# The 32x32 corner of a cross network's tail: from a padded weight tile to two small tiles read straight from the tail weights

## The chip, the cores and the metric

The kernel runs on one core of one Trainium2 chip. The metric is the device time of one execution in microseconds (us). The chip's engines are called PE (TensorE, matrix multiply; PEld is its loading of weights), DVE (VectorE), ACT (ScalarE), POOL (GpSimd) and SP (SyncE, which issues most of the DMAs).

## What is computed

```python
B, F, D, L = 4096, 26, 16, 6
Din = min(F * D, 1024)            # 416
...
def reference(x0, ws, bs):        # x0 [4096, 416], ws [6, 416, 416], bs [6, 416], all bf16
    x = x0
    for l in range(ws.shape[0]):
        x = x0 * (x @ ws[l] + bs[l]) + x
    return x
```

Since the bias enters every layer, the kernel keeps the state divided by x0 in its head: each layer's sum x @ W + b + (all earlier sums) + 1 stays in the accumulators (PSUM), and x is that sum times x0.

## The kernel before, in words

The state is held transposed, features on partitions. The 416 features are three chunks of 128 and a tail of 32 (DF = 384, DR = 32). The 4096 rows are taken in NS = 4 blocks of 1024 rows, and each block in two halves of 512 (h = 0, 1). For each block s and layer l the loop at the end of the kernel emits, in this order: the main matmuls of half 0 (`main`, 128x32 tiles: 128 rows of features, and the 32 output features of one quarter of a chunk in each of the four column strips), the tail block (`tail_rows`), the evictions of half 0 by VectorE (`leave`, L417), the tail outputs (`tail_outs`, from 384 main features to the 32 tail features), the tail's own eviction (`leave_tail`: ScalarE L427, a product on GpSimd L440, then swaps by ScalarE L404 and GpSimd L406), then the main matmuls and evictions of half 1. The last layer of the last block is done by rows of x and has no such tail block, so there are 23 of them.

The tail features are 32, a quarter of the partitions, so the tail of 1024 rows is folded: four groups q of G = 256 rows stand one above the other, group q on partitions 32q to 32q + 31 (`quad(q)`). Each tail tile has a second plane, in which neighbouring groups (q and q ^ 1) are swapped. With both planes a row group sees the two halves of 512 rows: even q takes both planes as one stretch of 512 columns, odd q takes them one after the other as two matmuls of 256.

`tail_rows` has two parts, each one step of the plan with one semaphore at its end. `first` holds row tiles (32x128: 32 tail features in, 128 features out) into the accumulators of chunks 0 and 1. `second` has the row tiles of chunk 2 on even groups and the corner, tail to tail, on odd groups. The corner multiplies by the 32x32 piece `wt_sb[..., DF:D]` of the tail weights; its outputs have to land on the partitions of the group whose rows they are. Before the change a padded copy does this: `wc_sb` holds, for each layer and each of two parts, a 32x128 tile that is zero but for the 32 columns of the wanted group, so that the corner too is a 32x128 matmul. The memset at L249 clears `wc_sb` and `corner` (L251) copies the pieces in on GpSimd: layer 0 ahead of the loop (L529), layer 1 after layer 0's tail (L561), layers 2 to 5 after layer 1's (L563). The accumulators of the tail are banks 6 and 7 (`T_BANK`): the partitions 0 to 63 of bank 6 and 64 to 127 of bank 7 are used.

The order of work is written by hand; the class `Plan` only derives the semaphores from the named reads and writes. All matmuls of the layers go through `mm` (L261, recorded as L262). `tail_in` transposes the next block's tail features into the upper columns of bank 6 in layer 2.

Of the kernel before, what the change touches and what calls it, by code (L numbers as in the profile page):

```python
# [118 lines left out]
def bass_standalone__dcn_v2_cross__recsys_kernel(  # L119
# [6 lines left out]
    B, D = x0.shape  # L126
    L = ws.shape[0]
    NC = 3
    DF = 128 * NC
# [5 lines left out]
    G = SB // 4  # L135
    JS = SB // 128
    NJ = B // 128
    T_BANK = (6, 7)
# [3 lines left out]
    with ExitStack() as es:  # L142

        def sb(name, shape, dt=BF16):
            return es.enter_context(nc.sbuf_tensor(name, shape, dt))

        w_sb = sb("w_sb", [128, L, NC, D])
        wt_sb = sb("wt_sb", [128, L, D])
        wc_sb = sb("wc_sb", [128, L, 2, 128])
        xin_sb = sb("xin_sb", [128, 4, D])  # L150
        xtl_sb = sb("xtl_sb", [128, NJ, DR])
        xr_sb = sb("xr_sb", [128, JS, D])
# [19 lines left out]
        ps = es.enter_context(nc.psum_tensor("ps", [128, 8, 512], FP32))  # L172
# [5 lines left out]
        P = Plan()  # L178

        def quad(q):  # L180
            return slice(32 * q, 32 * q + 32)
# [44 lines left out]
        for s in range(1, NS):  # L226
# [7 lines left out]
            writes=[("dummy",)],  # L234
# [3 lines left out]
                out=ident[:, :], in_=ones_sb[:, 0:128], pattern=[[-1, 128]],  # L238
# [6 lines left out]
                out=u_sb[:, :], in_=ones_sb[0:L + 1, 0:L], pattern=[[1, L]],  # L245
                compare_op=ALU.is_ge, fill=0.0, base=1, channel_multiplier=-1,
            ), reads=[("ones",)], writes=[("u",)],
        )
        P.add("gpsimd", lambda e: e.memset(wc_sb[:, :, :, :], 0.0), writes=[("wc", "wt%d" % i) for i in range(3)])  # L249

        def corner(a, b, name):  # L251
            for g in range(4):
                p = quad(g | 1)
                P.add(
                    "gpsimd", lambda e, p=p, g=g: e.tensor_copy(  # L255
                        out=wc_sb[p, a:b, g % 2, quad(g)], in_=wt_sb[p, a:b, DF:D]
                    ), reads=[("wt", name), ("wc", name)], writes=[("wc", name, g)], shifts=True,
                )


        def mm(pe, dst, lhsT, rhs, start, pos=None):  # L261
            return pe.matmul(  # L262
# [14 lines left out]
        def wkey(l):  # L277
            return "wt%d" % min(l, 2)
# [29 lines left out]
        def tail_rows(s, l, start):  # L308
            src, key = src_tail(s, l)
            keys = [("wt", wkey(l)), key, key + ("swapped",)]  # L310

            def rows(pe, q, h, m, begin):
                for part in range(2):
                    if q % 2 == 0:
                        if part:
                            break
                        dst, rhs = ps[:, bank(h, m), :], src[quad(q), :, :]
                    else:
                        dst, rhs = ps[:, bank(h, m), part * G:(part + 1) * G], src[quad(q), 1 - part, :]
                    ins = mm(  # L320
                        pe, dst, wt_sb[quad(q), l, m * 128:(m + 1) * 128], rhs, begin and part == 0, (32 * q, 0)
                    )
                return ins

            def first(pe):
                for q in range(4):
                    h, m = divmod(q, 2)
                    ins = rows(pe, q, h, m, l == 0 and h == 1)
                return ins

            def second(pe):
                for q in range(4):
                    h = q // 2
                    if q % 2 == 0:
                        ins = rows(pe, q, h, 2, l == 0 and h == 1)
                    else:
                        for part in range(2):
                            ins = mm(
                                pe, ps[:, T_BANK[h], 0:G], wc_sb[quad(q), l, part, :], src[quad(q), 1 - part, :],
                                start and part == 0, (32 * q, 0),  # L340
                            )
                return ins

            P.add("tensor", first, reads=keys, adds=[("ps", bank(h, m)) for h in HALVES for m in range(2)])
            P.add(
                "tensor", second, reads=keys + [("wc", wkey(l), g) for g in range(4)],
                adds=[("ps", bank(h, 2)) for h in HALVES] + [("ps", T_BANK[h]) for h in HALVES],
            )

# [17 lines left out]
        def tail_in(s):  # L367
            def fn(pe):
                for o in range(2 if s == 0 else 1):
                    for r in range(2):  # L370
                        for g in range(4):
                            j = 2 * (g ^ o) + r
                            src = xin_sb[:, j, DF:D] if s == 0 and j < 4 else xtl_sb[:, s * JS + j, :]
                            b, c = (7, o * G) if s == 0 else (T_BANK[0], G)
                            ins = mm(
                                pe, ps[quad(g), b, c + r * 128:c + (r + 1) * 128], src, ident[:, :],
                                s == 0 and o == 0 and r == 0, (0, 32 * g),
                            )
                return ins

            b = 7 if s == 0 else T_BANK[0]
            P.add(
                "tensor", fn, reads=[("ident",), ("xtl", 0 if s == 0 else 1)] + ([("xin", 0), ("xin", 1)] if s == 0 else []),
                adds=[("ps", b)],
            )
            if s == 0:
                P.add(
                    "scalar", lambda e: e.activation(  # L388
                        out=x0t_sb[:, s, :, :], in_=ps[:, 7, :].rearrange("p (o c) -> p o c", o=2), func=ACTF.Copy
                    ), reads=[("ps", 7)], writes=[("x0t", s), ("x0t", s, "swapped")],  # L390
                )
# [90 lines left out]
        for i in range(2):  # L482
            for c in CH:
                b = HEAD_BANKS[i][c]
# [10 lines left out]
                dst, src = x0T_sb[:, c, i * 256:(i + 1) * 256], psT[:, b, 0:256]  # L495
# [30 lines left out]
            )  # L526


        corner(0, 1, "wt0")  # L529
        for s in range(NS):  # L530
            for l in range(L):
                ending = s == NS - 1 and l == L - 2
                if s == NS - 1 and l == L - 1:
                    break
                if s == 0 and l == 0:
                    for k in CH:
                        for m in CH:
                            main(s, l, 0, m, k)
                        if k == 0:
                            bias_sums()  # L540
                        if k == 1:
                            tail_in(0)
                    tail_rows(s, l, True)
                    for c in CH:
                        leave(s, l, 0, c)
                    tail_outs(s, l, False)
                else:
                    for m in CH:
                        for k in CH:
                            main(s, l, 0, m, k)  # L550
                    tail_rows(s, l, l == 0)
                    for c in CH:
                        leave(s, l, 0, c)
                    tail_outs(s, l, False)
                if l == 2 and s < NS - 1:
                    tail_in(s + 1)
                leave_tail(s, l, not ending)
                if l == 2 and s < NS - 1:
                    keep_tail_in(s + 1)
                if s == 0 and l == 0:  # L560
                    corner(1, 2, "wt1")  # L561
                if s == 0 and l == 1:
                    corner(2, L, "wt2")  # L563
                if l == 1 and s > 0:
                    store_block(s - 1)
                if s < NS - 1 and l in (3, 4):
                    g = 2 * (l - 3)
                    swap(x0t_sb[:, s + 1], ("x0t", s + 1), tuple("scalar" if q // 2 == l - 3 else None for q in range(4)))
                if ending:
                    P.add(  # L570
                        "gpsimd", lambda e: e.tensor_tensor(
                            out=bt_sb[:, :], in0=cb_sb[:, NC, L - 1:L], in1=cb_sb[:, NC, L - 2:L - 1], op=ALU.subtract
                        ), reads=[("cb",)], writes=[("bt",)],
                    )
                    P.add(
                        "gpsimd", lambda e, t=t32_sb[:, l % 2, :]: e.tensor_scalar_add(st_sb[:, :], t, bt_sb[:, :]),
                        reads=[("t32", l % 2), ("bt",)], writes=[("st",)],
                    )
                    for c in CH:
                        keep_sum(0, c, "scalar")  # L580
                for m in CH:
                    for k in CH:
                        main(s, l, 1, m, k)
                    leave(s, l, 1, m)
                if ending:
                    for c in CH:
                        keep_sum(1, c, ("scalar", "scalar", "vector")[c])
            if s < NS - 1:
                transpose_block(s)
# [131 lines left out]
```

## Time and profile before

| | |
|---|---|
| runs, median (lowest to highest) | 129.16 us (128.88 to 129.17) |
| the profiled execution | 129.15 us, of which the span is 127.9 us |
| granted clock of TensorE | 1.00 |
| PE | busy 124.4 us, 2426 matmuls |
| DVE | busy 98.2 us |
| ACT | busy 50.1 us |
| POOL | busy 39.6 us |
| corner matmuls (wc_sb) | 92, 268 ns each |
| copies into wc_sb, memset | 12 of 0.2 to 0.3 us, 1.37 us |

The profile lists, for one execution, groups of instructions (line, engine, operation, output and inputs, shape of the tile as rows*columns, count), the waits between engines, the chain of work that ended last, and a timeline in which neighbouring instructions of one kind are merged into a line: its start, its length, and how many there are. The length of a matmul's record is not the time it occupies the engine: the records of a stream overlap, and their ends are modelled. What a matmul costs is read from the distance between the starts.

### The profile page before, as it was taken

To read this page: it belongs to the slowest core of one execution; us is meant where nothing else is said; L and a number is where in the kernel's file an instruction comes from. 1 tells how busy PE (TensorE), PEld (TensorE's weight loads), DVE (VectorE), ACT (ScalarE), POOL (GpSimd) and SP (SyncE) were. 2 spreads that over 40 slices of the span, in tenths; PEclk is the share of its full clock that TensorE was granted. 3 is DMA by queue.
4 is the path that set the end of the run, shared out by engine and by line. 5 is a ranking of instruction groups with operands and counts; after the bars stand their busy time and mean duration, and the time that the engine had idled before them with its cause. 6 is when DMAs were issued, how large, how long until landed. Compare 5 with 4: busy or idle time off the path is not lost.

```text
span 127.9 us, 5334 instructions
## 1 busy us (share of the span) xinstructions
PE 124.4 (97%) x2426; PEld 64.7 (51%) x2426; DVE 98.2 (77%) x150; ACT 50.1 (39%) x112; POOL 39.6 (31%) x88
## 2 busy tenths in 40 slices
PE   7999999999999999999999999999999999999991
PEld 5545445545545545545545545545555555455660
DVE  0329779679779779788788797797797797797973
ACT  1534226356405224354513243373422252253820
POOL 7025364034014053043122152241221351340550
PEclk9999999999999999999999999999999999999999
DMA  3987999997739307000019208000009606100016
GB/s 106 205 201 175 161 262 273 172 204 149 253 67 143 65 19 258 5 0 5 0 33 192 52 0 265 7 5 0 5 0 129 142 5 233 38 0 5 0 38 233
DMA packets 34054, 13.12 MB, mean 103 GB/s; under 512 B 25322, under 2 KB 34032, under 8 KB 34032
## 3 DMA queue, kind: packets, MB, share of 16 engines
q1 hardware_dynamic: 33328, 12.25, 45.8%
q10 hardware_dynamic: 704, 0.54, 1.3%
q8 instruction: 19, 0.31, 1.0%
q14 instruction: 3, 0.02, 0.0%
HBM read 4.07 MB, written 3.41 MB: 58 GB/s over the span
## 4 chain that ended last, share of the span: by engine, by line
PE 97%; ACT 0%; DVE 0%; issue 0%
PE ps L262 93%; PE ps L270 2%; PE ps L488 1%; ACT x0t_sb L388 0%; DVE o_sb L652 0%
## 5 line engine op out<-in xcount | busy, mean ns | idle before, releaser
L417 DVE SCALAR_TENSOR_TENSOR xT_sb<-ps,cb_sb,x0T_sb 128x512 bf16<-128x512 f32 x120 | 80.8, 743 | 19.5 <-PE ps L262 19.5
L262 PE MATMUL ps<-xT_sb,w_sb 128*32 128x512 bf16 (+1 forms) x1596 | 84.6, 364 | 0.0
L262 PEld LDWEIGHTS ps<-xT_sb,w_sb 128*32 128x32 bf16 x1596 | 40.8, 97 | 37.2 <-issue 4.0
L427 ACT ACTIVATE t_sb<-ps,cb_sb 64x256 f32<-64x256 f32 x46 | 21.6, 470 | 51.3 <-PE ps L262 51.0
L440 POOL TENSOR_TENSOR xt_sb<-t_sb,x0t_sb 128x256 bf16<-128x256 f32 x20 | 13.4, 672 | 64.1 <-ACT t_sb L427 64.1
L404 ACT ACTIVATE xt_sb<-xt_sb 32x256 bf16<-32x256 bf16 x38 | 15.7, 414 | 15.3 <-POOL xt_sb L440 15.1
L262 PE MATMUL ps<-x0T_sb,w_sb 128*32 128x512 bf16 (+1 forms) x336 | 18.9, 368 | 0.0
L406 POOL COPY xt_sb<-xt_sb 32x256 bf16<-32x256 bf16 x38 | 14.9, 392 | 2.4
L417 DVE SCALAR_TENSOR_TENSOR xo_sb<-ps,cb_sb,x0T_sb 128x512 bf16<-128x512 f32 x18 | 12.1, 743 | 2.5 <-PE ps L262 2.5
L262 PEld LDWEIGHTS ps<-x0T_sb,w_sb 128*32 128x32 bf16 x336 | 8.4, 97 | 7.6 <-issue 0.6
L262 PE MATMUL ps<-xt_sb,wt_sb 32*128 32x512 bf16 (+1 forms) x152 | 11.8, 326 | 0.0
L262 PE MATMUL ps<-xt_sb,wc_sb 32*128 32x256 bf16 x76 | 7.4, 268 | 0.0
L262 PEld LDWEIGHTS ps<-xt_sb,wt_sb 32*128 32x128 bf16 x152 | 2.5, 91 | 8.4 <-DVE xT_sb L417 6.4
L440 POOL TENSOR_TENSOR xot_sb<-t_sb,x0t_sb 128x256 bf16<-128x256 f32 x3 | 2.0, 672 | 9.9 <-ACT t_sb L427 9.9
L262 PE MATMUL ps<-w_sb,xT_sb 128*32 128x416 bf16 (+1 forms) x60 | 5.1, 339 | 0.0
L404 ACT ACTIVATE x0t_sb<-x0t_sb 32x256 bf16<-32x256 bf16 x12 | 4.9, 410 | 0.1
L652 DVE TENSOR_TENSOR o_sb<-ps,xr_sb 128x416 bf16<-128x416 f32 x6 | 3.4, 588 | 1.3 <-PE ps L262 1.0
L255 POOL COPY wc_sb<-wt_sb 32x32 bf16<-32x32 bf16 (+1 forms) x12 | 2.8, 233 | 4.7 <-DMA wt_sb<-in_ws_dram 4.1
L270 PE MATMUL ps<-const-bfloat16-1.0 128*128 128x256 bf16 x14 | 3.1, 418 | 0.8 <-PEq L706 0.8
L262 PEld LDWEIGHTS ps<-xt_sb,wc_sb 32*128 32x128 bf16 x76 | 3.7, 93 | 0.2
L503 DVE COPY x0T_sb<-ps 128x256 bf16<-128x256 bf16 x4 | 1.1, 292 | 3.4 <-PE ps L488 3.2
L449 ACT ACTIVATE sS_sb<-ps,cb_sb 128x512 bf16<-128x512 f32 x5 | 3.0, 692 | 0.0
(41 smaller groups left out, 33.6 us busy)
## 6 DMA issues: line engine op xcount, KB each, us to landing
out_dram<-o_sb SPq DMA_DIRECT2D x3, 832.0 KB, 4.4
w_sb<-in_ws_dram SPq DMA_DIRECT2D x5, 312.0 KB, 4.3
xr_sb<-in_x_dram SPq DMA_DIRECT2D x1, 832.0 KB, 5.3
wt_sb<-in_ws_dram SPq DMA_DIRECT2D x4, 104.0 KB, 2.9
out_dram<-o_sb SPq DMA_DIRECT2D x2, 208.0 KB, 2.2
w_sb<-in_ws_dram SPq DMA_DIRECT2D x3, 104.0 KB, 3.4
xin_sb<-in_x_dram ACTq DMA_DIRECT2D x1, 208.0 KB, 3.2
xin_sb<-in_x_dram SPq DMA_DIRECT2D x1, 208.0 KB, 2.9
```

The source lines that it names most:

```text
L255: "gpsimd", lambda e, p=p, g=g: e.tensor_copy(out=wc_sb[p, a:b, g % 2, quad(g)], in_=wt_sb[p, a:b, DF:D]), reads=[("wt", name), ("wc", nam ...
L262: return pe.matmul(dst, lhsT=lhsT, rhs=rhs, start=start, stop=True, skip_group_check=True, tile_position=pos,)
L270: ins = pe.matmul(ps[:, 7, 0:256], lhsT=const[:, 0:128], rhs=const, start=True, stop=True)
L404: fn = lambda e, d=dst, s=src: e.activation(out=d, in_=s, func=ACTF.Copy)
L406: fn = lambda e, d=dst, s=src: e.tensor_copy(out=d, in_=s)
L417: "vector", lambda e: e.scalar_tensor_tensor(out=dst, in0=ps[:, bank(h, c), :], scalar=cb_sb[:, c, l:l + 1], in1=x0T_sb[:, c, o:o + H], op ...
L427: "scalar", lambda e, p=p, h=h: e.activation(out=dst[p, :], in_=ps[p, T_BANK[h], 0:G], func=ACTF.Identity, bias=cb_sb[p, NC, l:l + 1]), re ...
L440: "gpsimd", lambda e: e.tensor_tensor(out=dst, in0=t, in1=x0t_sb[:, s, 0, :], op=ALU.mult),
L449: fn = lambda e: e.activation(out=o, in_=i, func=ACTF.Identity, bias=b)
L488: ins = pe.transpose(out=psT[:, b, j * 128:(j + 1) * 128], in_=xin_sb[:, 2 * i + j, c * 128:(c + 1) * 128], identity=ident[:, :],)
L503: "vector", lambda e, d=dst, s=src: e.tensor_copy(out=d, in_=s),
L652: "vector", lambda e: e.tensor_tensor(out=o_sb[:, jj, :], in0=ps[:, b, 0:D], in1=xr_sb[:, j, :], op=ALU.mult), reads=[("ps", b), ("xr",)], ...
```

## The change

The padded tile, its memset and its copies go. The corner is four 32x32 matmuls per tail block, whose weights are read straight from the tail weights: the tile position (32q, 32g) takes row group q as input and puts the result into the column strip of group g. In `second` the order of the groups becomes 0, 2, 1, 3, so that both row tiles of the even groups come before the four corner matmuls. As a corner matmul now writes only the 32 partitions of its group, and no longer zeros to the other 96, `tail_in` sets its start flag for the groups 2 and 3 of bank 6 itself.

```diff
-        wc_sb = sb("wc_sb", [128, L, 2, 128])
...
-        P.add("gpsimd", lambda e: e.memset(wc_sb[:, :, :, :], 0.0), writes=[("wc", "wt%d" % i) for i in range(3)])
-
-        def corner(a, b, name):
-            for g in range(4):
-                p = quad(g | 1)
-                P.add(
-                    "gpsimd", lambda e, p=p, g=g: e.tensor_copy(
-                        out=wc_sb[p, a:b, g % 2, quad(g)], in_=wt_sb[p, a:b, DF:D]
-                    ), reads=[("wt", name), ("wc", name)], writes=[("wc", name, g)], shifts=True,
-                )
...
             def second(pe):
-                for q in range(4):
+                for q in (0, 2, 1, 3):
                     h = q // 2
                     if q % 2 == 0:
                         ins = rows(pe, q, h, 2, l == 0 and h == 1)
                     else:
-                        for part in range(2):
+                        for o in range(2):
+                            g = q ^ o
                             ins = mm(
-                                pe, ps[:, T_BANK[h], 0:G], wc_sb[quad(q), l, part, :], src[quad(q), 1 - part, :],
-                                start and part == 0, (32 * q, 0),
+                                pe, ps[quad(g), T_BANK[h], 0:G], wt_sb[quad(q), l, DF:D], src[quad(q), o, :],
+                                start, (32 * q, 32 * g),
                             )
                 return ins
...
             P.add(
-                "tensor", second, reads=keys + [("wc", wkey(l), g) for g in range(4)],
+                "tensor", second, reads=keys,
...
-                                s == 0 and o == 0 and r == 0, (0, 32 * g),
+                                o == 0 and r == 0 and (s == 0 or g >= 2), (0, 32 * g),
...
-        corner(0, 1, "wt0")
...
-                if s == 0 and l == 0:
-                    corner(1, 2, "wt1")
-                if s == 0 and l == 1:
-                    corner(2, L, "wt2")
```

## The prediction

> **What bounds the kernel now.** I read the page's engine row first, then the chain that ended last, then the timeline of TensorE, and last the waits. Page, engine row and chain:
>
> ```profile
> PE 124.4 (97%) x2426; PEld 64.7 (51%) x2426; DVE 98.2 (77%) x150; ACT 50.1 (39%) x112; POOL 39.6 (31%) x88
> ...
> PE 97%; ACT 0%; DVE 0%; issue 0%
> PE ps L262 93%; PE ps L270 2%; PE ps L488 1%; ACT x0t_sb L388 0%; DVE o_sb L652 0%
> ```
>
> TensorE is busy for 97% of the span, and the chain is TensorE for 97%; its order in time shows one unbroken piece of line 262 from 8.27 us to 125.27 us. Granted clock is 1.00 there (view by stretches). So after 8.27 us whatever TensorE takes longer or shorter goes into the end one for one, unless another engine becomes late. VectorE, next in line, works six evictions of 743 ns per layer (4.46 us) in a layer period of 4.88 us (start of one tail block to the next, 57.43 to 62.31 us below).
>
> The question is the tail block, of which there are 23 (four blocks of 1024 rows by six layers, less the last layer, which is done by rows). Timeline of TensorE from 57 to 67.5 us, start and length in us:
>
> ```profile
> 57.98 4.40 PE L262 MATMUL ps<-xT_sb,w_sb 128*32 128x256 bf16 x84
> 62.31 0.60 PE L262 MATMUL ps<-xt_sb,wt_sb 32*128 32x512 bf16 x7
> 62.54 0.27 PE L262 MATMUL ps<-xt_sb,wc_sb 32*128 32x256 bf16 x1
> 62.54 0.37 PE L262 MATMUL ps<-xt_sb,wt_sb 32*128 32x512 bf16 x1
> 62.55 0.38 PE L262 MATMUL ps<-xt_sb,wc_sb 32*128 32x256 bf16 x3
> 62.86 2.45 PE L262 MATMUL ps<-xT_sb,w_sb 128*32 128x256 bf16 x48
> ```
>
> The reader is to see that the block lasts 0.55 us (62.31 to 62.86) and that the four wc matmuls cost no time of their own: they start at 62.54 and 62.55 with the row tiles of the even groups and run in the row groups that those leave free. The single records of this block, in ns from the first (62310): row tiles 0, 3, 10, 13, then the second halves of the odd groups at 123 and 133; the second part's row tiles of 512 columns at 226 and 236, wc at 232 and 242, and wc again at 341 and 351; the first main matmul at 549.
>
> **What a column costs.** Quartets of main matmuls without a change of shape start 215.7 ns apart at 512 columns and 109 ns at 256. The slope is 106.7/256 = 0.417 ns a column: 107 ns for 256 columns, 213 ns for 512, and some 2 ns besides.
>
> **What a change of tile shape costs.** The records start late wherever the next matmul has another tile shape than the one before. TensorE around the bias sums (128x32 tiles, then 7x32, then 128x32) and near the end (32x128, then 128x128):
>
> ```profile
> 5.87 0.38 PE L262 MATMUL ps<-x0T_sb,w_sb 128*32 128x512 bf16 x4
> 6.19 0.26 PE L262 MATMUL ps<-u_sb,bsa_sb 7*32 7x6 bf16 x16
> 6.37 0.40 PE L262 MATMUL ps<-x0T_sb,w_sb 128*32 128x512 bf16 x4
> ```
>
> ```profile
> 122.18 0.18 PE L262 MATMUL ps<-ident,st_sb 32*128 32x32 bf16 x4
> 122.30 0.53 PE L262 MATMUL ps<-w_sb,xT_sb 128*128 128x416 bf16 x2
> ```
>
> From the last record before, plus its columns, to the first after: 128x32 to 32x128, 61998 + 213 to 62310, 99 ns (98 or 99 in all 22 tail blocks that wait for nothing else); 32x128 to 128x32, 62661 + 107 to 62859, 91 ns (90 or 91 in all 23); 128x32 to 7x32, 5880 + 213 to 6189, 96 ns; 7x32 to 128x32, 6287 to 6377, some 88 ns (this one has a load to wait for too); 32x128 to 128x128, 122197 + 13 to 122302, 92 ns. Besides, the first round after a change is 10 to 12 ns longer: 120 instead of 109 ns (62859 to 62979), 226 instead of 216 ns (6377 to 6603). A tile of 7 rows by 32 columns in one strip of rows is the nearest that this trace has to a 32x32 tile.
>
> **The change part by part.** *The corner matmuls.* Four per block before and after, 256 columns each, four weight loads before and after. Their tile was 32x128, like the row tiles beside them; now it is 32x32. They come after both even row tiles, so the block gets one more change of shape, 32x128 to 32x32, and leaves from 32x32 instead of from 32x128. No change from 32x128 to 32x32 is in this trace. Bounds: at the one end it costs nothing and the corners run beside the 512-column row tiles, as wc does; at the other it costs what the dearest change costs, 99 ns, with nothing beside it. I take 92 ns, in the middle of the five kinds seen (88 to 99 ns), since every change of shape that the trace shows unmasked has it, whether the rows alone change (bias sums, 122.30 us) or rows and columns. That only the number of columns changes here is the weak point.
>
> Block after, in ns from its first record: even row tiles at 226 and 236 as before; their columns end at 236 + 213 = 449; the change, 92, gives 541; the four corners start 3 to 4 ns apart, the last at 551 (the four bias matmuls start at 6189, 6192, 6196, 6199); 107 for its columns and 11 for the first round after a change, 669; the change to the main tiles, 91, gives 760. Before it was 549: 211 ns longer. That the four corners share one stretch of 107 ns, though each has its own moving data, I take from the tail outputs of the 48 matmuls at 62.86 us: quartets with four different sources at 109 ns each. The price by the lowest and highest of the rows: gap in 90, no longer first round and a gap out of 65 (the 88 less the 23 to 25 ns that the small bias matmuls may themselves take) gives 236 + 213 + 90 + 10 + 107 + 65 = 721, 172 ns longer; gap in 99, corners spread over 14 ns and a first round of 12 gives 236 + 213 + 99 + 14 + 107 + 12 + 91 = 772, 223 ns longer. Over 23 blocks: 211 ns is 4.85 us, with 3.96 and 5.13 us as ends.
>
> *The Trainium skill* speaks on this from both sides, and the sum above needs neither. Its page "TensorEngine Tiling (Array Packing)", section "Key Properties", says that a change of tiling mode, and not only of the tile, drains TensorE; the gaps above agree for the changes they show, the page gives no price, and by it the corners would come out as in my sum, near 133.8 us. Its page "TensorE: Matmul & The Clock Gate", section "Part 3: Packing small matmuls — row/col tiling", says that weight loads overlap running matmuls when their row groups differ; read by itself that would let the corners of groups 1 and 3 run beside the row tiles of groups 0 and 2, and the sum would be near 128.8 us.
>
> *The copies that go.* GpSimd loses a memset (1.37 us) and twelve copies (2.8 us). Nearly all of it lies in GpSimd's idle time, between the swaps and the next product, which waits for ScalarE. Two of TensorE's waits name it:
>
> ```profile
> PEld ps L262 <- POOL wc_sb L255: 0.7, 2, 0.4
> ```
>
> That figure is idle time of the weight loads, partly behind matmuls. In the records, the block at 18.03 us has its second part 371 ns after its first instead of 226: it waits for the four copies of layers 2 to 5 (17.00 to 18.34 us). From the main quartet before to the first main matmul after, it lasts 1022 instead of 871 ns; the block at 13.15 us 877 instead of 871; the block at 8.27 us waits for ScalarE, not for the copies. Gain 0.151 + 0.006 = 0.157 us. Nothing takes the place of this wait: the first part of each block waits for the same tail weights already, and they had landed when the copies began (17.00 us at the latest, block at 18.03). Without the copies' wait the second part is bound by its row groups.
>
> *No cost and no gain:* the start flags in tail_in (same matmuls), the freed buffer, the new order of the second part. Its semaphore goes up some 0.2 us later within the block, but VectorE first works the two banks of the first part (1.49 us from 62.77 us), so the third bank is ready in time. The tail outputs, and behind them ScalarE's and GpSimd's tail chain, shift with TensorE; the swaps before the block at 62.31 us end at 61.85 us, and the period gets longer, not shorter. No DMA is moved.
>
> **Sum.** The profiled execution took 129.15 us (span 127.9 and 1.25 around it), the median of the runs is 129.16. 129.15 + 4.85 - 0.16 = 133.84; I say 133.8 us.
>
> **Rivals.** *The corners hide (not slower).* Place: the change from 32x128 to 32x32 in the second part. If it has no gap, the corners run in row groups 1 and 3 beside the 512-column tiles, and the block ends with those: 236 + 213 + 91 = 540 instead of 549. That gives 23 x 9 = 0.21 us and 0.16 from the copies, 128.8 us. For it: the row groups are free, wc does so today, and the trace has no unmasked change of columns alone. Against: five kinds of change, five gaps. It decides when a block grows by less than 7 ns (0.157 us / 23); from there on the kernel is slower.
>
> *The corners follow without a gap.* They wait for the row tiles, but the change is free: 107 ns a block, 2.46 us, 131.4 us. Against: no gap below 65 ns at any change in the records.
>
> *The two corners of one row group go one after the other.* Another 107 ns a block, 2.46 us: 136.3 us. Against: the tail outputs' quartets at 109 ns.
>
> *The change does nothing*, since wc is hidden now and only the 0.16 us are to be had: this is the first rival less its 9 ns, 129.0 us, and counted with it.
>
> **How the numbers follow.** Gaps as in my sum 0.78 (own range 133.0 to 134.2); follow without a gap 0.07; hidden 0.12; one after the other 0.03. The range goes from 131.4 to 134.5 us: it takes in the first two and leaves out the last two, 0.15, and a little of my own case. A measurement can tell about 0.3% (0.39 us) from no change; 128.8 lies just on this edge, so of the 0.12 I give 0.04 to faster and 0.08 to the same; slower 0.88.
>
> **What would show it.** Right: in each block the corner matmuls, as 32*32 tiles, start some 300 ns after the even row tiles (62.54 us today for both), and the next main matmul some 0.21 us after the four; block length 0.76 instead of 0.55 us; layer period 5.09 instead of 4.88 us; clock at 1.00; no block at 18 us with a longer stretch than its neighbours. Wrong: corners that start within 20 ns of the even row tiles (hidden), at 215 ns after them (no gap), or in two steps 107 ns apart (one after the other). VectorE's idle time should grow by some 0.2 us a layer; if TensorE instead waits for VectorE or ScalarE, the one-for-one step was wrong.

## The result, and the profile after

The changed kernel takes 134.06 us (median of 6 runs, 133.5 to 134.13) against 129.25 us (6 runs, 128.88 to 129.65): a ratio of 1.0347, 95% interval 1.0321 to 1.0373. The forecast was 133.8 us, the range 131.4 to 134.5. The profiled execution took 134.10 us, its span 132.8 us (before 129.15 and 127.9), the clock 1.00 in both.

Page of the changed kernel: engine row, chain and VectorE's evictions (busy, mean ns, idle before and its releaser); below it the evictions of the kernel before. The lines that were L262 and L417 are now L250 and L406.

```profile
PE 128.3 (97%) x2426; PEld 61.8 (47%) x2426; DVE 98.1 (74%) x150; ACT 50.0 (38%) x112; POOL 35.5 (27%) x75
...
PE 92%; DMA 3%; SPq 1%; ACT 0%; DVE 0%; issue 0%
...
L406 DVE SCALAR_TENSOR_TENSOR xT_sb<-ps,cb_sb,x0T_sb 128x512 bf16<-128x512 f32 x120 | 80.9, 743 | 24.1 <-PE ps L250 24.1
```

```profile
L417 DVE SCALAR_TENSOR_TENSOR xT_sb<-ps,cb_sb,x0T_sb 128x512 bf16<-128x512 f32 x120 | 80.8, 743 | 19.5 <-PE ps L262 19.5
```

The same 2426 matmuls, and TensorE as full as before at 97%: a busy share says nothing of a stall between matmuls, since the records overlap. VectorE does the same work and waits longer for TensorE (24.1 us; 19.5 before), so TensorE is still what everybody waits for. The chain now begins with a load of the head (DMA 3%), which is another matter, below.

The tail block, timeline of TensorE (start, length):

```profile
64.64 0.83 PE L250 MATMUL ps<-xt_sb,wt_sb 32*128 32x512 bf16 x12
65.40 2.45 PE L250 MATMUL ps<-xT_sb,w_sb 128*32 128x256 bf16 x48
```

It lasts 0.76 us, 0.55 before. All twelve matmuls are merged into one line, and the line bears the name of the first form only. A window that begins behind the ends of the row tiles' records shows the corners by themselves, here for TensorE and then for its weight loads; the third view is of the weight loads before:

```profile
65.18 0.29 PE L250 MATMUL ps<-xt_sb,wt_sb 32*32 32x256 bf16 x4
65.40 0.29 PE L250 MATMUL ps<-xT_sb,w_sb 128*32 128x256 bf16 x4
```

```profile
65.18 0.10 PEld L250 LDWEIGHTS ps<-xt_sb,wt_sb 32*32 32x32 bf16 x4 [0.42 <-issue]
65.40 0.12 PEld L250 LDWEIGHTS ps<-xT_sb,w_sb 128*32 128x32 bf16 x8
```

```profile
62.30 0.12 PEld L262 LDWEIGHTS ps<-xt_sb,wt_sb 32*128 32x128 bf16 x8 [0.42 <-DVE xT_sb L417]
62.43 0.21 PEld L262 LDWEIGHTS ps<-xt_sb,wc_sb 32*128 32x128 bf16 x4
62.85 0.23 PEld L262 LDWEIGHTS ps<-xT_sb,w_sb 128*32 128x32 bf16 x12 [0.21 <-issue]
```

The four corners start at 65.18, 0.3 us behind the even row tiles (64.87), and the main matmuls 0.22 us behind them. Their loads too come only at 65.18, after 0.42 us in which no weights were loaded and nothing that the profile names was waited for ("issue"). Before, the corners' loads (wc_sb) began at 62.43, while row tiles ran. Single records, ns from the block's first:

```
                        rows, 1st part    odd, 2nd half   even rows, 2nd part   corner               main
before (62.31 us)       0 3 10 13         123 133         226 236               232 242 341 351      549
after  (64.64 us)       0 3 10 13         122 132         226 236               540 544 547 550      759
```

Over the 23 blocks the time from a block's first record to the first main matmul sums to 12.786 us before and 17.450 after, 4.664 us more. All else behind the first block is the same: the 22 stretches between blocks 95.57 and 95.58 us, and from the last block's end to the start of the last matmul 8.41 us in both. The first block starts at 8.27 and 8.45 us. So the 4.9 us in the span are 4.66 from the blocks and 0.18 from the head, with rounding.

### The profile page after: what moved, and what is told of

Its sections match the earlier page's. It is cut to its first block, busy times and chain, and to the rows that moved or that the text cites. A ratio compares the mean times of both kernels' runs of the same rounds, so it can differ in the third digit from the quotient of the medians.

```text
span 132.8 us, 5313 instructions
## 1 busy us (share of the span) xinstructions
PE 128.3 (97%) x2426; PEld 61.8 (47%) x2426; DVE 98.1 (74%) x150; ACT 50.0 (38%) x112; POOL 35.5 (27%) x75
## 4 chain that ended last, share of the span: by engine, by line
PE 92%; DMA 3%; SPq 1%; ACT 0%; DVE 0%; issue 0%
PE ps L250 92%; DMA xtl_sb<-in_x_dram 3%; SPq L187 1%; ACT x0t_sb L377 0%; DVE o_sb L636 0%
## 5 line engine op out<-in xcount | busy, mean ns | idle before, releaser
L406 DVE SCALAR_TENSOR_TENSOR xT_sb<-ps,cb_sb,x0T_sb 128x512 bf16<-128x512 f32 x120 | 80.9, 743 | 24.1 <-PE ps L250 24.1
L250 PE MATMUL ps<-xT_sb,w_sb 128*32 128x512 bf16 (+1 forms) x1596 | 84.6, 364 | 0.0
L250 PEld LDWEIGHTS ps<-xT_sb,w_sb 128*32 128x32 bf16 x1596 | 40.8, 97 | 35.5
L250 PE MATMUL ps<-x0T_sb,w_sb 128*32 128x512 bf16 (+1 forms) x336 | 18.6, 365 | 0.2 <-DVE x0T_sb L492 0.2
L250 PE MATMUL ps<-xt_sb,wt_sb 32*128 32x512 bf16 (+2 forms) x228 | 15.7, 310 | 0.0
L406 DVE SCALAR_TENSOR_TENSOR xo_sb<-ps,cb_sb,x0T_sb 128x512 bf16<-128x512 f32 x18 | 12.1, 744 | 3.1 <-PE ps L250 3.1
L250 PEld LDWEIGHTS ps<-x0T_sb,w_sb 128*32 128x32 bf16 x336 | 8.4, 97 | 7.3 <-DVE x0T_sb L492 0.4
L250 PEld LDWEIGHTS ps<-xt_sb,wt_sb 32*128 32x128 bf16 (+1 forms) x228 | 4.2, 90 | 16.1 <-issue 16.1
L250 PE MATMUL ps<-w_sb,xT_sb 128*32 128x416 bf16 (+1 forms) x60 | 5.1, 339 | 0.0
L250 PE MATMUL ps<-x0t_sb,wt_sb 32*128 32x512 bf16 (+2 forms) x48 | 3.3, 310 | 0.1
L250 PEld LDWEIGHTS ps<-w_sb,xT_sb 128*32 128x32 bf16 (+1 forms) x60 | 2.2, 97 | 1.4 <-issue 0.2
L647 POOL TENSOR_TENSOR o_sb<-f_sb,xr_sb 128x416 bf16<-128x416 f32 x2 | 1.9, 974 | 2.9 <-ACT f_sb L643 2.9
```

The source lines that it names most:

```text
L250: return pe.matmul(dst, lhsT=lhsT, rhs=rhs, start=start, stop=True, skip_group_check=True, tile_position=pos,)
L406: "vector", lambda e: e.scalar_tensor_tensor(out=dst, in0=ps[:, bank(h, c), :], scalar=cb_sb[:, c, l:l + 1], in1=x0T_sb[:, c, o:o + H], op ...
L647: "gpsimd", lambda e: e.tensor_tensor(out=o_sb[:, jj, :], in0=t, in1=xr_sb[:, j, :], op=ALU.mult),
```

## The experiments

The two theories throughout: a change of tile shape stalls TensorE for some 92 ns, adds 11 ns to its first round, and nothing runs across it; or it is the small corner tiles themselves, their order or their columns that cost.

**Alternating: three changes more.** The changed kernel with

```diff
-                for q in (0, 2, 1, 3):
+                for q in range(4):
```

> The changed kernel with the groups of the second part in the order 0, 1, 2, 3, so that row tiles and corners alternate: three changes of tile shape more per tail block than the kernel before, instead of one. Theory (every change costs a gap of some 92 ns, makes the first round 11 ns longer, and nothing runs across it): first record of the second part at 226, columns to 439, corners at 531, to 653, row tile at 744, to 967, corners at 1059, to 1180, main matmuls at 1271 ns; 722 ns more than the 549 of before, 23 blocks, less 0.16 us: 145.6 us. Rival (the 32x32 tiles themselves cost the 210 ns a block, in whatever order they stand): 134.0 us, as the changed kernel.

Measured 145.68 us, ratio 1.126 (1.1199 to 1.1321). Timeline of TensorE, then of the weight loads, in one block:

```profile
58.89 1.34 PE L250 MATMUL ps<-xt_sb,wt_sb 32*128 32x512 bf16 x12
60.16 1.59 PE L250 MATMUL ps<-xT_sb,w_sb 128*32 128x256 bf16 x32
```

```profile
59.42 0.30 PEld L250 LDWEIGHTS ps<-xt_sb,wt_sb 32*32 32x32 bf16 x3 [0.41 <-issue]
59.94 0.09 PEld L250 LDWEIGHTS ps<-xt_sb,wt_sb 32*32 32x32 bf16 x2 [0.23 <-issue]
60.16 3.90 PEld L250 LDWEIGHTS ps<-xT_sb,w_sb 128*32 128x32 bf16 x84
```

A block of 1.27 us, with two separate bursts of corner loads (59.42 and 59.94; the third load of the first burst is the second row tile's, merged into its line). The records: even row tile 226, corners 530 and 534, second row tile 744, corners 1058 and 1061, main 1270 in 20 of 23 blocks and 1269 in three; forecast 531, 744, 1059, 1271. The same twelve matmuls take 511 ns longer than in the changed kernel (1270 against 759), only by their order, and 721 longer than the block before (forecast 722). The rival is out.

**Corners of 8 columns.** The changed kernel with

```diff
             def second(pe):
+                n = G if l == 0 else 8
...
-                                pe, ps[quad(g), T_BANK[h], 0:G], wt_sb[quad(q), l, DF:D], src[quad(q), o, :],
+                                pe, ps[quad(g), T_BANK[h], 0:n], wt_sb[quad(q), l, DF:D], src[quad(q), o, 0:n],
```

> The changed kernel with corner matmuls of 8 instead of 256 columns in layers 1 to 5 (248 columns of each corner product are left out, in 19 of the 23 blocks). Theory: the gap stays and only the columns go: corners at 541 to 551, some 3 to 25 ns for their columns, 11 for the first round, 91 out, main matmuls at 656 to 680 ns, 107 to 131 ns more than before; with four blocks of 210 ns, less 0.16 us: 131.9 to 132.3 us. Rival (the corners' columns are the whole cost, the gap is only how the records look): 19 blocks at about 549 ns, 129.9 us.

Measured 131.71 us, ratio 1.0202 (1.0127 to 1.0277). The corners start at 540 to 551 as in the changed kernel, and the main matmuls at 654 to 656 ns in the 19 short blocks, at 758 or 759 in the four whole ones. One short block, starting at 58.22 us, behind the row tiles' records:

```profile
58.76 0.18 PE L250 MATMUL ps<-xt_sb,wt_sb 32*32 32x8 bf16 x4
58.87 0.40 PE L250 MATMUL ps<-xT_sb,w_sb 128*32 128x256 bf16 x8
```

So of the 210 ns, 107 are left when the columns are all but gone, and 103 went with the columns: a half each.

**Order alone.** The kernel before, padded tile and all, with

```diff
             def second(pe):
-                for q in range(4):
+                for q in (0, 2, 1, 3):
```

> The kernel before, with its padded tile and copies, but the second part in the order 0, 2, 1, 3. Theory (order alone costs nothing, since no shape changes and the row groups are independent): block 549 ns, 129.0 to 129.4 us. Rival (corners that stand behind both even row tiles wait for them, whatever their shape): corners at 440 ns or later, block some 100 to 210 ns longer, 131.5 to 134.0 us.

Measured 129.25 us, ratio 1.0002 (0.9967 to 1.0037): no change, blocks of 548 to 550 ns but for the one at 17.7 us that waits for the copies (699). The corners run beside the even tiles as they did, the first two at 231 to 242 ns. Standing behind both row tiles is no cost; having another shape is.

**One shape.** The changed kernel with the row tiles cut up too, and groups 0, 2, 1, 3 in both parts:

```diff
-                    ins = mm(
-                        pe, dst, wt_sb[quad(q), l, m * 128:(m + 1) * 128], rhs, begin and part == 0, (32 * q, 0)
-                    )
+                    for c in range(4):
+                        f0 = m * 128 + 32 * c
+                        ins = mm(
+                            pe, dst[quad(c)], wt_sb[quad(q), l, f0:f0 + 32], rhs, begin and part == 0, (32 * q, 32 * c)
+                        )
...
             def first(pe):
-                for q in range(4):
+                for q in (0, 2, 1, 3):
```

> The changed kernel with all row tiles of the tail block cut into four 32x32 tiles as well (36 matmuls a block where there were 12; even groups first in both parts): the block has one shape, so no change inside it, and no padded tile. Theory (only changes of shape cost): the corners run beside the even groups' tiles again; sixteen tiles start some 3.4 ns apart, even groups end at about 23 + 226 + 213 = 462, main matmuls at about 553 ns, 129.1 us; up to 129.8 if the 36 starts do not all hide. Rival (small tiles are the cost): far above, at 134 us or more.

Measured 131.50 us, ratio 1.0162 (1.0101 to 1.0224). The expectation failed: better than the changed kernel, so small tiles are not the cost, but 2.4 us above the forecast of 129.1 and 1.7 above its upper end. In the profile 22 of the blocks take 641 to 643 ns (one takes 1163, see below), since the corners start at 411, 419, 428 and 436 ns, though the last row tile starts at 250 and their row groups are free by about 290 (the last second half of an odd group starts at 182, and 256 columns take 107). One block, starting at 58.72 us, behind the row tiles' records:

```profile
59.13 0.30 PE L250 MATMUL ps<-xt_sb,wt_sb 32*32 32x256 bf16 x4
59.36 0.51 PE L250 MATMUL ps<-xT_sb,w_sb 128*32 128x256 bf16 x11
```

The corners are the last 4 of 36 matmuls. Two readings: what comes after 32 matmuls arrives late, or the corners themselves wait. The next two runs part them.

**28 matmuls.** As the run with one shape, but an odd group takes its 512 columns in one matmul per tile:

```diff
...
+                    rhs = src[quad(q), :, :] if q % 2 == 0 else src[quad(q), ::-1, :]
...
```

> As the run with one shape, but the odd groups' row tiles take their 512 columns as one matmul each (the two planes read in reverse order): 28 instead of 36 matmuls in a tail block. In that run the corners, the last 4 of 36, started at 411 to 436 ns, some 160 ns after the last row tile, though their row groups were free from about 290. Theory (supply: some 32 matmuls with their loads wait ready at the start of the block, what comes after these arrives late): all 28 are ready, corners at about 255 to 280 ns, block 553 ns, 129.1 us. Rival (the corners themselves wait 160 ns for the last row tile): corners at about 410, block 630 to 640 ns, 131.0 us.

Measured 129.34 us (12 executions, 128.60 to 131.72), ratio 1.0004 (0.9970 to 1.0037). Corners at 252 to 280 ns, beside the even row tiles, and blocks of 553 to 555 ns. Timeline of TensorE:

```profile
63.01 0.62 PE L250 MATMUL ps<-xt_sb,wt_sb 32*32 32x512 bf16 x28
63.56 2.45 PE L250 MATMUL ps<-xT_sb,w_sb 128*32 128x256 bf16 x48
```

The block is at 0.55 us again with 32x32 corners read straight from the tail weights, and with no padded tile and no copies: what the change was to do costs nothing that these runs can tell (blocks of 554 instead of 549 ns, and no copies to wait for) once the block has one shape and 28 matmuls.

**Corners ahead of the row tiles.** The run with one shape and

```diff
             def second(pe):
-                for q in (0, 2, 1, 3):
+                for q in (1, 3, 0, 2):
```

> As the run with one shape and 36 matmuls, but in the second part the corners come ahead of the row tiles, so that the last four of the 36 are row tiles of group 2. Theory (supply): corners at about 280 ns, and the last four row tiles at 411 to 436 ns, as the corners before; with 213 ns for their columns and 91 out the block is 740 ns, 133.4 us. Rival (the corners themselves wait): the last four row tiles start by 300 ns, and the block ends with the corners or with them at 640 ns or less, 131.2 us.

Measured 133.57 us, ratio 1.0358 (1.0304 to 1.0411). The corners start at 256 to 292 ns, and now four row tiles start at 411, 419, 427 and 436; blocks of 748 to 750 ns (forecast 740). One block, starting at 58.96 us, behind the other records:

```profile
59.38 0.41 PE L250 MATMUL ps<-xt_sb,wt_sb 32*32 32x512 bf16 x4
59.71 0.40 PE L250 MATMUL ps<-xT_sb,w_sb 128*32 128x256 bf16 x8
```

Whatever stands at places 33 to 36 is late. The rival is out.

**Short matmuls first.** The run with one shape and

```diff
             def first(pe):
-                for q in (0, 2, 1, 3):
+                for q in (1, 3, 0, 2):
```

> As the run with one shape and 36 matmuls, but the first part begins with the odd groups, so that the block's first matmul has 256 instead of 512 columns (its record ends at about 278 instead of 385 ns). In the two runs with 36 matmuls the 33rd started at 411 ns. Theory (a window: the 33rd may only enter when the oldest matmul has ended, 26 ns later): corners at about 305 to 330 ns; even row tiles of the second part start by about 300, so the block is about 300 + 213 + 91 = 605 ns, 130.3 us. Rival (the 33rd comes a fixed 411 ns after the block's start, whatever is ahead): corners at 411, block 641 ns, 131.1 us.

Measured 131.14 us, ratio 1.0163 (1.0106 to 1.0219): the time fits the rival, the blocks do not. Corners at 305, 313, 321 and 330 ns, blocks of 606 to 608 ns (forecast 305 and 605) but for the first (616) and the seventh. In the profiled execution (130.85 us) the seventh lasts 1227 ns; without these 0.62 us it would be at 130.2, the forecast 130.3. The other executions left no trace, so what puts the median another 0.3 us above the profiled one is not known. Single stops of this kind stand in three of the four kernels with more matmuls: 0.52 us in the seventh block of the run with one shape, and with 28 matmuls 0.37 us between main matmuls (477 ns between two starts, where 109 is usual), after which the halves of each quartet run apart, so that the next block begins 0.48 us late in all. Timeline of TensorE in the run with 28 matmuls and in this one, with the idle time and its releaser in brackets:

```profile
23.92 0.39 PE L250 MATMUL ps<-xT_sb,w_sb 128*32 128x256 bf16 x6
24.52 0.72 PE L250 MATMUL ps<-xT_sb,w_sb 128*32 128x256 bf16 x12 [0.20 <-issue]
```

```profile
37.82 0.67 PE L250 MATMUL ps<-x0t_sb,wt_sb 32*32 32x256 bf16 x31
38.73 0.39 PE L250 MATMUL ps<-x0t_sb,wt_sb 32*32 32x512 bf16 x5 [0.24 <-issue]
```

TensorE waits for nothing that the profile names. These kernels have 6049 or 6417 instructions instead of 5313, and 22 or 23 packets of the instruction queue instead of 19; that the stops are instructions arriving late is a guess that no run tested. The traces fit it: the run with one shape and this one stop ahead of the same matmul of the program, the 854th, and the last packet of the instruction queue before each of the three stops ended 1.26 to 1.43 us before TensorE went on (37.80 and 39.06 us with one shape, 23.23 and 24.52 with 28 matmuls, 37.30 and 38.73 here). With the corners ahead of the row tiles, where nothing stops, that packet ended 1.75 us before the same place of the program (37.09 and 38.84).

**The corner in the main tiles' shape.** Per layer and group a weight tile of 128x32 that is zero but for the group's 32 rows (a memset and four copies on GpSimd, as before); the corners leave `second` and stand at the head of `tail_outs`:

```diff
...
+                for g in range(4):
+                    mm(pe, ps[quad(g), T_BANK[g // 2], 0:G], wd_sb[:, l, g, :], srct[:, 0, :], l == 0, (0, 32 * g))
                 for k in CH:
```

> The corner in the shape of the main tiles: a 128x32 weight tile per group that is zero but for the group's own 32 rows, four matmuls of 256 columns at the head of the tail outputs, where 128x32 tiles follow anyway. The corner is out in the open, but no shape changes for it. Theory: the tail block ends with the even row tiles, 236 + 213 + 91 = 540 instead of 549 ns, and one quartet of 256 columns, 109 ns, is added: 100 ns a block, 2.30 us, and the copies are waited for 0.5 us later, so their 0.16 us go: 131.3 us. Rival (a corner that does not hide costs 210 ns in any shape): 133.8 us.

Measured 131.32 us, ratio 1.0163 (1.0121 to 1.0205). One block:

```profile
58.56 0.61 PE L261 MATMUL ps<-xt_sb,wt_sb 32*128 32x512 bf16 x8
59.10 0.29 PE L261 MATMUL ps<-xt_sb,wd_sb 128*32 128x256 bf16 x4
59.22 4.38 PE L261 MATMUL ps<-xT_sb,w_sb 128*32 128x256 bf16 x84
```

The blocks end at 540 ns and the quartet adds 109 (0.12 us in this view, with the longer first round after the change of shape). A corner in the open costs its columns and no more, if no shape changes for it.

**The copies' wait.** The kernel before, the copies of layer 2 ahead of those of layers 3 to 5:

```diff
...
-                    corner(2, L, "wt2")
+                    corner(2, 3, "wt2", "c2")
+                    corner(3, L, "wt2", "c3")
```

> The kernel before with the copies of layer 2 ahead of those of layers 3 to 5 (two steps of four copies instead of one): the copies that the block at 18 us waits for end some 0.3 us sooner. Theory (the wait on them costs 0.15 us once, and nothing takes its place): that block 871 to 877 instead of 1022 ns from the main quartet before to the main matmul after, all others as they are; 129.0 us, a ratio of 0.999, less than the interval can tell. Rival (something else is as late): the block stays above 950 ns.

Measured 129.07 us, ratio 0.9985 (0.9962 to 1.0009), which can't be told from no change. In the profile the block at 18.1 us takes 871 ns from the main quartet before to the main matmul after, 1022 before, and the waits keep one of the two:

```profile
PEld ps L262 <- POOL wc_sb L255: 0.4, 1, 0.4
```

(0.7 us, 2 times, before.) The sum of the 23 blocks falls by 0.162 us; nothing took the wait's place. Whether this version is faster than the kernel before the runs do not settle.

## Why the prediction was right

**The bound.** That TensorE's time goes into the end one for one held: 4.66 us in the blocks, and nothing in the 22 stretches between. VectorE's idle time before its two groups of evictions (L417, now L406) went from 22.0 to 27.2 us (19.5 + 2.5 to 24.1 + 3.1), 0.23 us a layer, some 0.2 in the forecast.

**The stall, from kinds of change that were not this one.** Forecast for a block: corners at 541 to 551, main at 760, 211 ns more. Measured: 540 to 551, main at 759, 210 ns more. The weak point, that only the columns of the tile change here, did not matter: 236 + 213 to 541 is the same 92 ns as where the rows change, in both directions (run with alternating groups). The Trainium skill, "TensorEngine Tiling (Array Packing)", "Key Properties", says that a change of mode drains TensorE. All the changes in these runs agree, with 88 to 99 ns for it. The skill's rule that weight loads overlap running matmuls when their row groups differ stands in "TensorE: Matmul & The Clock Gate", "Part 3: Packing small matmuls — row/col tiling". Here the overlap is seen between tiles of one shape (wc loads at 124 to 244 ns of the block, first corners at 231 to 280 ns), and not across a change of shape: the 32x32 corners' loads come at 539 ns, though row groups 1 and 3 are free from about 240 (133 + 107).

**One stretch for the four corners.** Their starts are 3 to 4 ns apart and main follows after 208 ns, 107 + 11 + 91 as in the sum: they run side by side. The run with 8 columns separates the 103 ns that 248 columns take from the rest.

**The copies.** Forecast 0.157 us; 0.162 in the run with split copies. No other wait came up. There was more room than the prediction says: the swaps that the block at 62.31 us reads ended at 61.15 us, and 61.85 is the end of ScalarE's swaps for the next rows.

**The rivals.** "Hidden" is what happens with one shape and 28 matmuls (129.34), not with the change. "Without a gap" comes near the price of the corner in the main shape: 131.32, where 131.4 was worked out for 107 ns of exposed columns a block; that kernel pays 109 and saves 9.

**What was not in the sum.** 133.84 against 134.10 us in the profile. The blocks and the copies together, 4.85 - 0.16 = 4.69, measured 4.66; the rest is the head, where the first block began 0.18 us later because a load landed later (the chain's DMA piece), and 0.10 us that lies outside the span (134.10 less 132.76 us, against 129.15 less 127.90). In the eleven profiles that first block starts anywhere from 7.92 to 8.62 us, with and without the copies, so I count it as scatter of the loads and not as the change's. The range had room for it.

## What to carry to other kernels

Count the changes of tile shape (rows and columns alike) along TensorE's stream, and price each by the same kernel's own gaps: about 100 ns here, and everything that used to run beside the moved matmul is exposed as well. A padded tile that keeps its neighbours' shape can be cheaper than a small tile with less work; if the small tile is wanted, cut its neighbours to the same shape, and count the matmuls between two changes: 28 hid here, and of 36 the last four came late.

## What the runs showed of the hardware that was not expected

- **A change of columns alone stalls as much** as one of rows: 92 ns from 32x128 to 32x32 and 92 back (alternating run: 534 + 107 + 11 to 744), beside 88 to 99 ns for the five kinds in the trace of before.
- **Matmuls start out of program order across row groups.** The program has group 1's second half (256 columns) ahead of group 2's row tile; on the chip group 2 starts at 10 ns and group 1's second half at 123 ns, when its own row group is free.
- **The 33rd matmul behind a change of shape comes late, by as much as the first one is long.** With a first matmul of 512 columns (record ends at 385 ns) the 33rd starts at 411 ns, in two orders of the work; with one of 256 columns (278 ns) at 305 ns, 26 and 27 ns after the record's end. The ends are modelled; by the starts alone the 33rd comes 106 ns sooner when the first matmul is 256 columns (107 ns) shorter. So it looks as if some 32 matmuls with their weight loads are ready ahead and the 33rd enters when the oldest has ended. The next follow 8 ns apart, where ready ones start 3.4 ns apart; why is not known. Among main matmuls it would not show: 32 of them are eight quartets, some 0.9 to 1.7 us by the distances of 109 and 215.7 ns.
